# The last group's first layer as seven products of quarters, with shared sums passed between PSUM banks

## The chip, the cores and the metric

The kernel runs on one core of one Trainium2 chip. Its engines work side by side and meet only at semaphores: TensorE (PE, matrix products; PEld is its weight load), VectorE (DVE), ScalarE (ACT), GpSimd (POOL) and SyncE (SP), whose queues also issue transfers. The metric is the time of one execution on the device in microseconds. TensorE writes its products into PSUM, which has eight banks of 512 f32 values per partition; VectorE and ScalarE read them from there and also can write there. SBUF is the working memory.

## What is computed

An attention with a window of 128 tokens and a linear bias (8 batches, 8 heads, 576 tokens, head size 64), whose output is the input of a normalisation and a two-layer network with a residual:

```python
scores = scale * np.matmul(q, k.transpose(0, 1, 3, 2))
mask = (rel >= 0) & (rel < window)
scores = np.where(mask, scores + bias[None], -1000000000.0)
attn = softmax(scores)
x = (attn @ v).transpose(0, 2, 1, 3).reshape(B, S, H * D)    # 8 x 576 x 512

mu, var = x.mean(-1), ((x - mu) ** 2).mean(-1)
xn = (x - mu) / np.sqrt(var + 1e-06) * g_ln
out = x + np.maximum(xn @ w_ch1, 0.0) @ w_ch2                # 512 -> 2048 -> 512
```

## The kernel before

The 8 x 576 tokens are cut into 36 blocks of 128: two batches form a pair, a pair has nine blocks, and block 8 of a pair holds the two 64-token tails (T = 8). The blocks go through the network in groups: four groups of two blocks and then seven of four (groups 4 to 10). Group 10, the last one, has four blocks, 512 tokens.

TensorE's work is written out in order by hand. `weave_at` runs the generator of one layer of one group and, at listed places, lets attention steps of later blocks in between (scores, exponentials, masks, products with v, centring, transposes). Within a queue every engine works in the order of the program. The last group has no attention left to weave in.

**First layer (`mlp1`, L724).** The centred input stands transposed in `turned_x[g]` as four row blocks (NKB = 4) of 512 tokens. For each of 16 column blocks of w1 (NFB = 16), four matmuls of 512 columns accumulate into one PSUM bank (L734), and ScalarE (L750) or, for blocks 6 and 13 of a group, VectorE (L742) writes the ReLU of it to `ht_all` as f16. `w1g` is w1 with the gain of the normalisation multiplied in. Dividing by the standard deviation is left to the end (`rstd`, from `inv_std`, L590, nine small VectorE steps in a chain).

**Second layer by seven products (`mlp2_seven`, L813, and `mlp2_last`, L892).** From group 4 on the product of the hidden layer and w2 is made from seven products of quarters in place of eight. The hidden layer A is cut into quarters by tokens and by hidden blocks, w2 (B) by hidden blocks and by output columns. Four sums of quarters of A (`sum_hidden`, L794, on VectorE, into `hsums`) and four of B (`sum_w2`, once) enter the products. Some products accumulate on top of others in one bank: the bank is read by `onto` (scaled by `rstd` and added to the output) and then the next product is added to what is in it. A sum that two quarters of the output share is made in this way once. For the last group `mlp2_last` does the same per half of the tokens (`pair`), in pieces of 256 columns: 14 products of 8 matmuls (L905), each followed by an `onto` (L919) and, where a half row of the output is complete, by a store.

The places where `sum_hidden` runs during the first layer are in `SUMS_AT` (by unit of the first layer). The last group's `inv_std` runs after unit 1 of its first layer.

**PSUM.** Two score tiles take four banks (`ps_scores`), and a pool of four buffers (`ps_mm`) serves everything else. **Buffers.** `raw_pool` has four buffers each for q and k as loaded (1024 f16 values per partition), `turned_pool` holds them transposed (four for q, five for k). Once the last block's attention is done, none of them is used any more.

Of the kernel before, what the change touches and what calls it, by code (L numbers as in the profile page):

```python
# [53 lines left out]
}  # L54

FAR = 60000.0


# [20 lines left out]
def kernel(  # L79
# [21 lines left out]
    def pool(name, bufs, **kw):  # L101
        return ctx.enter_context(tc.tile_pool(name=name, bufs=bufs, **kw))

    consts = pool("consts", 1)
    raw_pool = pool("raw", 4)
    turned_pool = {"q": pool("turned_q", 4), "k": pool("turned_k", 5)}
# [4 lines left out]
    group_pool = pool("group", 3)  # L111
    out_pool = pool("outp", 5)
    sums_pool = pool("sums", 1)
    ps_scores = pool("ps_scores", 1, space=PSUM)
    ps_mm = pool("ps_mm", 4, space=PSUM)


    iden_dram = nc.inline_tensor(np.eye(P, dtype=np.float16), name="iden16")
# [605 lines left out]
    def mlp1(g, on_dve=()):  # L724
        xT = turned_x[g]
        w = w1 if g < FIRST_GROUPS else w1g
        cols = len(members[g]) * P

        at = g % 2 * cols if len(members[g]) == 2 else 0
        ht = hidden[g] = ht_all[:, :, at : at + cols]  # L730
        for fb in range(NFB):
            ps = ps_mm.tile([P, 4 * P], FP32, tag="mm", name="ps_m1")
            for kb in range(NKB):
                nc.tensor.matmul(  # L734
                    ps[:, 0:cols],
                    w[:, kb, fb * P : (fb + 1) * P],
                    xT[:, kb, 0:cols],
                    start=(kb == 0),
                    stop=(kb == NKB - 1),
                )  # L740
            if fb in on_dve:
                nc.vector.tensor_scalar(  # L742
                    out=ht[:, fb, :],
                    in0=ps[:, 0:cols],
                    scalar1=0.0,
                    scalar2=None,
                    op0=ALU.max,
                )
            else:
                nc.scalar.activation(  # L750
                    out=ht[:, fb, :], in_=ps[:, 0:cols], func=AF.Relu
                )
            yield cols
# [29 lines left out]
    def minus(out, a, b, op=ALU.subtract):  # L783
        nc.vector.tensor_tensor(out=out, in0=a, in1=b, op=op)  # L784

    def sum_w2(i):
# [2 lines left out]
        out, a, b = [(t1, b12, b11), (t3, b22, b12), (t2, b22, t1), (t4, b21, t2)][i % 4]  # L789
        minus(out[:, c], a[:, c], b[:, c])  # L790

    hsums = {}
# [99 lines left out]
    def mlp2_last(g):  # L892


        ht = hidden[g]
        s = [hsums.pop((g, i)) for i in (1, 2, 3, 4)]
        a11, a12, a22 = ht[:, 0:half], ht[:, half:NFB], ht[:, half:NFB]
        outs = {}

        def quarter():  # L900
            return ps_mm.tile([P, DM], FP32, tag="mm", name="ps_q")[:, 0 : DM // 2]

        def product(ps, lhs, at, rhs, first):
            for fb in range(half):
                nc.tensor.matmul(  # L905
                    ps,
                    lhs[:, fb, at : at + P],
                    rhs[:, fb, :],
                    start=(first and fb == 0),
                    stop=(fb == half - 1),  # L910
                    skip_group_check=True,
                )

        def onto(ps, at, cols, fresh):
            p, blk = members[g][at]
            n = p * NSLOT + blk
            if at not in outs:
                outs[at] = out_pool.tile([P, DM], FP32, tag="o", name="o")
            nc.vector.scalar_tensor_tensor(  # L919
                out=outs[at][:, cols],  # L920
                in0=ps,
                scalar=rstd[:, n : n + 1],
                in1=(xs[p, blk] if fresh else outs[at])[:, cols],
                op0=ALU.mult,
                op1=ALU.add,
            )

        x = {}
        for pair in range(2):
            x[pair] = quarter()  # L930
            product(x[pair], a11, pair * P, b11, True)
            onto(x[pair], pair, left, True)
            yield
        for pair in range(2):
            t = quarter()
            product(t, a12, pair * P, b21, True)
            onto(t, pair, left, False)
            yield
        for pair in range(2):
            top, low = pair, 2 + pair  # L940
            at = pair * P
            product(x[pair], s[1], at, t2, False)
            onto(x[pair], top, right, True)
            yield
            y = quarter()
            product(y, s[0], at, t1, True)
            onto(y, low, right, True)
            yield
            product(x[pair], s[2], at, t3, False)
# [3 lines left out]
            product(y, s[3], at, b22, False)  # L953
            onto(y, top, right, False)
            store(*members[g][top], outs[top])
# [16 lines left out]
        )  # L972
        store(p, blk, o)

    def store(p, blk, o, cols=slice(0, DM)):
        n = p * NSLOT + blk
        for b, t0, w, p0 in spans(p, blk):
            dst, src = out[b, t0 : t0 + w, cols], o[p0 : p0 + w, cols]
            if blk == T:
                last = n >= count - 4 and b % 2 == 1  # L980
                (nc.scalar if last else nc.sync).dma_start(out=dst, in_=src)
            else:
                dst = dst.rearrange("(c r) d -> r c d", r=2)
                last = n >= count - 4
                for r in range(2):
                    (nc.scalar if last and r else nc.sync).dma_start(
                        out=dst[r], in_=src[r * HALF : (r + 1) * HALF]
                    )

    def weave_at(units, *places, seven=None, sums=None):  # L990


        advance_to(done + places.count(-1))
        for u, _ in enumerate(units):
            if seven is not None:
# [18 lines left out]
    with tc.manual_schedule(engines={engine.PE}):  # L1014
        with tc.manual_schedule(engines={engine.Activation, engine.DVE, engine.SP, engine.Pool}):
            advance_to(first)
            weave_at(mlp1(0, (0, 1)), 2, 7, 8, 9, 13)
            weave_at(mlp1(1), 2, 8, 12)
            weave_at(mlp2(0, ((0, 8), (8, 12), (12, NFB))), 1, 4, 8, 10, 10, 12)
            weave_at(mlp2(1), 1, 3, 5, 7, 9, 13, 13)  # L1020
            weave_at(mlp1(2), 0, 4, 7, 9, 14)
            weave_at(mlp2(2), 1, 5, 9, 13, 13, 15, 15)

            weave_at(mlp1(3, (9, 10, 11)), 4, 7, 8, 10, 12, 15, sums=0)
            weave_at(mlp2(3), 0, 2, 3, 6, 9, 11, sums=4)
            for g in range(4, len(GROUPS)):
                one, two = LEAD[g - 4]
                weave_at(mlp1(g, (6, 13) if one else ()), *one, seven=g)  # L1030
                last = g == len(GROUPS) - 1
                weave_at((mlp2_last if last else mlp2_seven)(g), *two)
    assert done == len(steps)


# [28 lines left out]
```

## Time and profile before

| | |
|---|---|
| median of three runs | 309.07 us (309.05 to 312.04) |
| profiled execution | 309.11 us, span 307.3 us |
| TensorE busy | 299.2 us, 97% of the span |
| VectorE / ScalarE / GpSimd busy | 231.7 / 182.2 / 111.9 us |
| last group's first layer | 277.10 to 290.91 us |
| last group's second layer | 290.91 to 303.30 us |
| last VectorE instruction | ends at 303.82 us |

Times in the rows are microseconds from the start of the span, and a row of the timeline gives start, length, engine, line, operation, tiles, shape and count; in square brackets stands the idle time of the engine before it and what ended that. A row of the groups gives the count, the busy time, the mean length of one in ns, and the idle time before them. Since matmuls are pipelined, the length of one is longer than its share of the time: what a matmul costs in a row is the distance between starts.

### The profile page before, as it was taken

To read this page: it belongs to the slowest core of one execution; us is meant where nothing else is said; L and a number is where in the kernel's file an instruction comes from. 1 tells how busy PE (TensorE), PEld (TensorE's weight loads), DVE (VectorE), ACT (ScalarE), POOL (GpSimd) and SP (SyncE) were. 2 spreads that over 40 slices of the span, in tenths; PEclk is the share of its full clock that TensorE was granted. 3 is DMA by queue.
4 is the path that set the end of the run, shared out by engine and by line. 5 is a ranking of instruction groups with operands and counts; after the bars stand their busy time and mean duration, and the time that the engine had idled before them with its cause. 6 is when DMAs were issued, how large, how long until landed. Compare 5 with 4: busy or idle time off the path is not lost.

```text
span 307.3 us, 9098 instructions
## 1 busy us (share of the span) xinstructions
PE 299.2 (97%) x3734; PEld 198.9 (65%) x3734; DVE 231.7 (75%) x624; ACT 182.2 (59%) x327; POOL 111.9 (36%) x152
## 2 busy tenths in 40 slices
PE   8889999999999999999999999999999999999994
PEld 2468755856754578647855786568646864784583
DVE  2688878789986799669867986798679867963563
ACT  7588775768967862675268536753685368305600
POOL 8923648583775372484117350750000000000000
PEclk9999999999999999999999999999999999999999
DMA  9999999999999999999999999994741161005004
GB/s 112 165 206 200 190 159 143 200 116 122 154 123 189 146 132 134 217 152 139 117 182 123 110 134 162 127 151 77 139 89 34 20 138 35 19 19 137 0 19 120
DMA packets 149851, 38.02 MB, mean 124 GB/s; under 512 B 140721, under 2 KB 145457, under 8 KB 149810
## 3 DMA queue, kind: packets, MB, share of 16 engines
q0 software_dynamic: 103744, 18.36, 87.4%
q1 hardware_dynamic: 45586, 18.56, 36.6%
q8 instruction: 29, 0.48, 0.7%
q10 hardware_dynamic: 480, 0.52, 0.5%
q14 instruction: 12, 0.10, 0.1%
HBM read 36.90 MB, written 9.44 MB: 151 GB/s over the span
## 4 chain that ended last, share of the span: by engine, by line
PE 89%; DMA 4%; POOL 3%; ACT 1%; issue 1%; DVE 0%; POOLq 0%
PE ps_m L734 39%; PE ps_s L826 25%; PE ps_m L764 9%; PE ps_sc L418 6%; DMA w<-in_moe_w_ch_dram 4%; PE ps_sc L500 4%; PE ps_q L905 4%; POOL vx L246 1%; POOL q L211 1%; POOL w L172 1%; POOL k L211 1%; PE ps_pv L471 1%; PE ps_tr L305 1%; PE ps_tx L571 1%; PE ps_sc L305 0%
## 5 line engine op out<-in xcount | busy, mean ns | idle before, releaser
L734 PE MATMUL ps_m<-xT,w1g 128*128 128x512 f16 (+1 forms) x576 | 117.8, 356 | 0.1
L750 ACT ACTIVATE ht_all<-ps_m 128x512 f16<-128x512 f32 (+1 forms) x159 | 81.2, 519 | 38.0 <-PE ps_m L734 36.0
L734 PEld LDWEIGHTS <-w1g 128*128 128x128 f16 x576 | 53.9, 98 | 49.9 <-issue 0.3
L426 ACT ACTIVATE probs<-ps_sc 128x1024 f16<-128x1024 f32 x56 | 56.5, 1029 | 46.2 <-PE ps_sc L418 46.2
L246 POOL DMA_DIRECT2D vx<-in_v_dram x40 | 34.0, 860 | 64.2 <-PE ps_sc L500 38.7
L826 PE MATMUL ps_s<-w,s 128*128 128x256 f16 x384 | 43.8, 273 | 0.0
L826 PEld LDWEIGHTS <-s 128*128 128x128 f16 x384 | 36.7, 98 | 4.7
L437 DVE TENSOR_TENSOR probs<-probs,m 128x1024 f16<-128x1024 f16 x56 | 36.9, 683 | 2.8 <-ACT probs L426 2.8
L826 PE MATMUL ps_s<-w,ht_all 128*128 128x256 f16 x288 | 34.3, 273 | 0.0
L784 DVE TENSOR_TENSOR s<-ht_all 128x1024 f16<-128x1024 f16 (+2 forms) x35 | 20.4, 583 | 18.1 <-ACT ht_all L750 17.5
L764 PE MATMUL ps_m<-w,ht_all 128*128 128x512 f16 x128 | 31.4, 380 | 0.0
L826 PEld LDWEIGHTS <-ht_all 128*128 128x128 f16 x288 | 27.3, 98 | 5.0
L235 POOL DMA_DIRECT2D q<-in_q_dram x40 | 27.5, 702 | 5.6 <-DMA vx<-in_v_dram 2.4
L847 DVE SCALAR_TENSOR_TENSOR o<-ps_s,rstd,x 128x256 f32<-128x256 f32 x48 | 21.0, 478 | 10.5 <-PE ps_s L826 10.5
L418 PE MATMUL ps_sc<-q,k 64*64 64x128 f16 (+1 forms) x1088 | 24.1, 210 | 1.0 <-ACT probs L426 0.8
L418 PEld LDWEIGHTS <-k 64*64 64x64 f16 x1088 | 15.8, 107 | 13.0 <-issue 10.5
L582 ACT ACTIVATE junk<-xc 128x512 f16<-128x512 f16 x28 | 17.6, 628 | 5.7 <-DVE xc L551 5.6
L232 POOL DMA_DIRECT2D k<-in_k_dram x20 | 18.0, 915 | 6.3 <-DMA k<-k 5.0
L509 DVE SCALAR_TENSOR_TENSOR x<-ps_sc,rec 128x512 f16<-128x512 f32 x28 | 19.4, 691 | 1.0
L847 DVE SCALAR_TENSOR_TENSOR o<-ps_s,rstd,o 128x256 f32<-128x256 f32 x36 | 15.7, 478 | 4.2 <-PE ps_s L826 4.0
L764 PEld LDWEIGHTS <-ht_all 128*128 128x128 f16 x128 | 11.1, 98 | 10.8
L500 PEld LDWEIGHTS <-probs 128*128 128x128 f16 x352 | 14.6, 98 | 3.5
(88 smaller groups left out, 327.1 us busy)
## 6 DMA issues: line engine op xcount, KB each, us to landing
out_dram<-o SPq DMA_DIRECT2D x66, 128.0 KB, 2.4
k<-in_k_dram POOLq DMA_DIRECT2D x32, 128.0 KB, 7.2
vx<-in_v_dram POOLq DMA_DIRECT2D x32, 128.0 KB, 7.1
w<-in_moe_w_ch_dram POOLq DMA_DIRECT2D x8, 512.0 KB, 10.9
q<-in_q_dram POOLq DMA_DIRECT2D x48, 64.0 KB, 6.1
q<-in_q_dram POOLq DMA_DIRECT2D x12, 128.0 KB, 7.7
k<-in_k_dram POOLq DMA_DIRECT2D x8, 64.0 KB, 6.8
vx<-in_v_dram POOLq DMA_DIRECT2D x8, 64.0 KB, 5.8
```

The costliest lines, as they stand in the source:

```text
L235: nc.gpsimd.dma_start(out=t[half, b], in_=tokens.rearrange("h (c r) d -> r c h d", r=2)[r],)
L246: nc.gpsimd.dma_start(out=vx[p0 : p0 + n, :, 0:D], in_=v[b, :, t0 : t0 + n, :].rearrange("h p d -> p h d"),)
L418: nc.tensor.matmul(in_halves(ps[cols, j, n, t, :])[:, r, queries], kt[rows, hp, cols], in_halves(qt[rows, b, hp])[:, r, queries], start=Tr ...
L426: nc.scalar.activation(out=dst.rearrange("p (n j) q -> p j n q", j=2), in_=ps.rearrange("p j n t q -> p j n (t q)"), func=AF.Exp, scale=in ...
L437: nc.vector.tensor_tensor(out=dst, in0=dst, in1=mask, op=ALU.mult)
L500: nc.tensor.matmul(ps[:, h, 0 : D + 1], pr[:, h, t, :], vext[(p * NSLOT + o) % NV][:, h, :], start=(n == 0), stop=(n == len(terms) - 1),)
L734: nc.tensor.matmul(ps[:, 0:cols], w[:, kb, fb * P : (fb + 1) * P], xT[:, kb, 0:cols], start=(kb == 0), stop=(kb == NKB - 1),)
L750: nc.scalar.activation(out=ht[:, fb, :], in_=ps[:, 0:cols], func=AF.Relu)
L764: nc.tensor.matmul(sums[at], ht[:, fb, at * P : (at + 1) * P], w2[:, fb, :], start=(fb == 0), stop=(fb == NFB - 1),)
L784: nc.vector.tensor_tensor(out=out, in0=a, in1=b, op=op)
L826: nc.tensor.matmul(ps[:, pair, :], lhs[:, fb, at : at + P], rhs[:, fb, :], start=(first and pair == 0 and fb == 0), stop=(fb == half - 1), ...
L847: nc.vector.scalar_tensor_tensor(out=outs[at][:, cols], in0=ps[:, pair], scalar=rstd[:, n : n + 1], in1=(xs[p, blk] if fresh else outs[at] ...
```

## The change

The last group's first layer is now made of seven products of quarters as well (`mlp1_last` replaces `mlp1` there). A is w1 (with gain), cut by input rows (row blocks 0, 1 and 2, 3) and by hidden columns (low and high 1024); B is the transposed input, cut by input rows and by tokens (256 and 256). A unit u is two of the eight column blocks of a half; it makes both its blocks of either half of the hidden layer, for all tokens. Each product of a unit is two blocks times two row blocks, four matmuls of 256 columns, into one bank. Per unit there are seven products, 28 matmuls, and there are four units.

- `a1`: a11 b11 into a bank x; ScalarE copies x into a second bank t (PSUM to PSUM).
- `a2`: a product of sums into a bank y; ScalarE copies y to SBUF as f32 (`copied`).
- `b`: a product of sums on top of x; VectorE writes x + copied to a bank s. A product on top of t completes the first quarter; ScalarE writes its ReLU.
- `c`: a product of sums on top of x; VectorE writes x + copied to `ht_all` (`out`, not yet clipped). A product on top of s completes the second quarter; ReLU on ScalarE (units 0, 2) or VectorE (units 1, 3).
- `d`: a product on top of x completes the third quarter; ReLU on ScalarE. VectorE clips the fourth in place, and then makes `sum_hidden` 1 and 2 for the unit.

x has three banks in turn, y one, t and s two each: all eight. For this the scores' banks are given back before the last group, and the pool `ps_mm` is opened first.

w1's eight sums (four for each of two row blocks, 128x1024 f16) are made on VectorE in groups 7, 8 and 9, into the raw buffers of q and k. The four sums of the input (128x512 f16) and `inv_std` come during the second layer of group 9, after units 20, 24 and 26.

In the second layer the order changes: the first product goes between `c` and `d` of the first layer's last unit, the four products with sums 1 and 2 come for both halves of the tokens before those with sums 3 and 4, and `sum_hidden` 3 and 4 run during it, in halves (128x1024). Each half row of the first two blocks is stored when it is done, the first halves from SP alone.

```diff
+W1_SUMS_AT = {
+    7: ({}, {25: 0}),
+    8: ({5: 4, 8: 1, 11: 5}, {25: 2}),
+    9: ({5: 6, 8: 3, 11: 7}, {}),
 }
...
+    def sum_w1(i):
+        kb, which = i // 4, i % 4 + 1
+        t = raw_pool.tile([P, FFN // 2], FP16, tag="qk"[kb], name="w1s")
+        w1sums[which, kb] = t
+        a11, a21 = w1g[:, kb, 0 : FFN // 2], w1g[:, kb, FFN // 2 :]
+        a12, a22 = w1g[:, 2 + kb, 0 : FFN // 2], w1g[:, 2 + kb, FFN // 2 :]
+        if which == 1:
+            minus(t, a21, a22, ALU.add)
+        elif which == 2:
+            minus(t, w1sums[1, kb], a11)
+        elif which == 3:
+            minus(t, a11, a21)
+        else:
+            minus(t, a12, w1sums[2, kb])
...
+    def mlp1_last(g, between, ps_last):
...
+        def a1(u):
+            product(x_of[u % 3], u, (0, 0), b11, True)
+            nc.scalar.copy(out=t_of[u % 2], in_=x_of[u % 3])
+
+        def a2(u):
+            product(y, u, 1, xsums[1], True)
+            c = turned_pool["q"].tile([P, 8 * P], FP16, tag="q", name="c")
+            copied[u] = c.bitcast(FP32)
+            nc.scalar.copy(out=copied[u], in_=y)
+
+        def b(u):
+            product(x_of[u % 3], u, 2, xsums[2], False)
+            minus(s_of[u % 2], x_of[u % 3], copied[u], ALU.add)
+            product(t_of[u % 2], u, (2, 0), b21, False)
+            nc.scalar.activation(out=out(u, 0, 0), in_=two(t_of[u % 2]), func=AF.Relu)
+
+        def c(u):
+            product(x_of[u % 3], u, 3, xsums[3], False)
+            minus(out(u, 1, 1), two(x_of[u % 3]), two(copied[u]), ALU.add)
+            product(s_of[u % 2], u, 4, b22, False)
+            if u % 2:
+                at_least_0(out(u, 0, 1), two(s_of[u % 2]))
+            else:
+                nc.scalar.activation(out=out(u, 0, 1), in_=two(s_of[u % 2]), func=AF.Relu)
+
+        def d(u):
+            product(x_of[u % 3], u, (2, 1), xsums[4], False)
+            nc.scalar.activation(out=out(u, 1, 0), in_=two(x_of[u % 3]), func=AF.Relu)
+            at_least_0(out(u, 1, 1), out(u, 1, 1))
+            units = 2 * u, 2 * u + 2
+            sum_hidden(g, 1, units)
+            sum_hidden(g, 2, units)
...
+        a1(0)
+        a2(0)
+        a1(1)
+        b(0)
+        a2(1)
+        a1(2)
+        for u in range(n):
+            if 0 < u < n - 1:
+                if u > 1:
+                    a1(u + 1)
+                a2(u + 1)
+            c(u)
+            if u < n - 1:
+                b(u + 1)
+            else:
+                between()
+            d(u)
...
+                if g == last - 1:
+                    late[20] = [(sum_x, last, i) for i in (1, 2)]
+                    late[24] = [(sum_x, last, i) for i in (3, 4)]
+                    late[26] = [(inv_std, sum(GROUPS[:last]), len(members[last]))]
...
+            units = mlp2_last(last)
+            scores_psum.close()
+            ps_last = pool("ps_last", 1, space=PSUM)
+            LAST_SUMS_AT = {
+                u: [(sum_hidden, last, 3 + u % 2, (c, c + half // 2))]
+                for u, c in ((2, 0), (4, half // 2), (3, 0), (5, half // 2))
+            }
+            mlp1_last(last, lambda: next(units), ps_last)
+            weave_at(units, more=LAST_SUMS_AT)
```

More of the change, by code (lines that the diff above doesn't have):

```diff
@@ L102, in pool @@
         return ctx.enter_context(tc.tile_pool(name=name, bufs=bufs, **kw))
+    ps_mm = pool("ps_mm", 4, space=PSUM)
     consts = pool("consts", 1)
@@ new lines, in mlp1_last, with product, two, out @@
+    def mlp1_last(g, between, ps_last):
+        xT = turned_x[g]
+        mid = 2 * P
+        ht = hidden[g] = ht_all
+        b11, b21, b22 = xT[:, 0:2, 0:mid], xT[:, 2:4, 0:mid], xT[:, 2:4, mid:]
+        *x_of, y = (
+            ps_last.tile([P, 4 * P], FP32, name=f"ps_x{i}", tag=f"ps_x{i}") for i in range(4)
+        )
+        t_of, s_of = (
+            [ps_mm.tile([P, 4 * P], FP32, tag="mm", name=f"ps_{n}") for _ in range(2)]
+            for n in "ts"
+        )
+        copied = {}
+        def product(ps, u, kbs, rhs, fresh):
+            for j in range(2):
+                for kb in range(2):
+                    fb = 2 * u + j
+                    if isinstance(kbs, tuple):
+                        first, low = kbs
+                        w = w1g[:, first + kb, (8 * low + fb) * P :][:, 0:P]
+                    else:
+                        w = w1sums[kbs, kb][:, fb * P : (fb + 1) * P]
+                    nc.tensor.matmul(
+                        ps[:, j * mid : (j + 1) * mid],
+                        w,
+                        rhs[:, kb, :],
+                        start=(fresh and j == 0 and kb == 0),
+                        stop=(kb == 1),
+                        skip_group_check=True,
+                    )
+        def two(ps):
+            return ps.rearrange("p (f c) -> p f c", f=2)
+        def out(u, low, second):
+            return ht[:, 8 * low + 2 * u : 8 * low + 2 * u + 2, second * mid : (second + 1) * mid]
+        def a1(u):
[17 more added lines that the diff above has]
+                at_least_0(out(u, 0, 1), two(s_of[u % 2]))
+            else:
+                nc.scalar.activation(out=out(u, 0, 1), in_=two(s_of[u % 2]), func=AF.Relu)
[6 more added lines that the diff above has]
+            sum_hidden(g, 2, units)
+        def at_least_0(out, ps):
+            nc.vector.tensor_scalar(
+                out=out, in0=ps, scalar1=0.0, scalar2=None, op0=ALU.max
+            )
+        n = NFB // 4
+        a1(0)
[12 more added lines that the diff above has]
+                b(u + 1)
+            else:
+                between()
+            d(u)
@@ L937, in mlp2_last @@
             onto(t, pair, left, False)
+            store(*members[g][pair], outs[pair], left, (nc.sync, nc.sync))
+            yield
+        y = {}
+        for pair in range(2):
+            top, low = pair, 2 + pair
+            at = pair * P
+            product(x[pair], hsums[g, 2], at, t2, False)
+            onto(x[pair], top, right, True)
+            yield
+            y[pair] = quarter()
+            product(y[pair], hsums[g, 1], at, t1, True)
+            onto(y[pair], low, right, True)
             yield
@@ L941, in mlp2_last @@
             at = pair * P
[L942 to L949, printed above, removed]
+            product(x[pair], hsums[g, 3], at, t3, False)
             onto(x[pair], low, right, False)
@@ L952, in mlp2_last @@
             yield
-            product(y, s[3], at, b22, False)
-            onto(y, top, right, False)
-            store(*members[g][top], outs[top])
+            product(y[pair], hsums[g, 4], at, b22, False)
+            onto(y[pair], top, right, False)
+            store(*members[g][top], outs[top], right)
             yield
@@ L979, in store, with weave_at @@
             if blk == T:
-                last = n >= count - 4 and b % 2 == 1
-                (nc.scalar if last else nc.sync).dma_start(out=dst, in_=src)
+                two[b % 2].dma_start(out=dst, in_=src)
             else:
                 dst = dst.rearrange("(c r) d -> r c d", r=2)
-                last = n >= count - 4
                 for r in range(2):
-                    (nc.scalar if last and r else nc.sync).dma_start(
+                    two[r].dma_start(
                         out=dst[r], in_=src[r * HALF : (r + 1) * HALF]
                     )
-    def weave_at(units, *places, seven=None, sums=None):
+    def weave_at(units, *places, seven=None, sums=None, more={}):
         advance_to(done + places.count(-1))
         for u, _ in enumerate(units):
+            for f, *args in more.get(u, []):
+                f(*args)
             if seven is not None:
```

36 lines of the change are left out of this document (28 added, 8 removed).

## The prediction

> **What bounds the kernel now.** I read the head of the page first, then the end of the chain of waits, then the last 30 us on the timeline and by windows.
>
> ```profile
> span 307.3 us, 9098 instructions
> PE 299.2 (97%) x3734; PEld 198.9 (65%) x3734; DVE 231.7 (75%) x624; ACT 182.2 (59%) x327; POOL 111.9 (36%) x152
> ...
> 268.53 8.73 PE ps_s L826 x80
> 277.26 13.81 PE ps_m L734 x64
> 291.07 12.24 PE ps_q L905 x112
> 303.34 0.48 DVE o L919
> ...
> 277.10:290.91 13.81, 13.81 (x67) 6.25 (x64) 6.17 (x18) 8.96 (x15) 0.00 (x0) 1.00 0.33 76
> 290.91:303.30 12.39, 12.39 (x113) 10.85 (x111) 8.08 (x18) 0.60 (x1) 0.00 (x0) 1.00 0.16 44
> ```
>
> TensorE is busy for 97% of the span, and the chain ends in TensorE alone: the last group's first layer (L734), its second (L905), one VectorE instruction and the stores. The windows (columns: length, PE, PEld, DVE, ACT, POOL, granted clock) show both layers without a TensorE gap at full clock. In the first, VectorE works 6.17 us of 13.81 and ScalarE 8.96; that is the room the change spends. The profiled execution took 309.11 us, its span 307.3; the median of the runs is 309.07, so I sum against 309.11.
>
> **The products.** Each form's price is its spacing in a long row.
>
> ```profile
> 290.91 3.66 PE L905 MATMUL ps_q<-w,ht_all 128*128 128x256 f16 x32
> 294.40 3.66 PE L905 MATMUL ps_q<-w,s 128*128 128x256 f16 x32
> ...
> L905 PEld LDWEIGHTS <-s 128*128 128x128 f16 x64 | 6.3, 98 | 0.7
> ```
>
> First layer before: 64 matmuls of 512 columns in 13.81 us, 0.2158 each. After: 7 products x 16 matmuls of 256 columns = 112. That form takes (294.40 - 290.91)/32 = 0.109 us, and its 98 ns weight load fits beneath. 112 x 0.1092 = 12.23 us, a saving of **1.58 us** if TensorE never waits. The second layer keeps its 112 matmuls and its last three products in the same order, so the tail behind the last product stays.
>
> **w1's sums.** Eight VectorE sums of 128x1024 f16 go into groups 7 to 9, 0.60 us of queue each (0.69 long, overlapping the next by about 0.09). They stand just ahead of these idle times:
>
> ```profile
> 217.24 0.88 DVE L847 SCALAR_TENSOR_TENSOR o<-ps_s,rstd,x 128x256 f32<-128x256 f32 x2 [1.28 <-PE ps_s L826]
> 226.07 0.69 DVE L784 TENSOR_TENSOR s<-ht_all 128x1024 f16<-128x1024 f16 x1 [1.20 <-ACT ht_all L750]
> 228.66 0.56 DVE L784 TENSOR_TENSOR s<-ht_all 128x768 f16<-128x768 f16 x1 [0.70 <-ACT ht_all L750]
> 248.48 0.88 DVE L847 SCALAR_TENSOR_TENSOR o<-ps_s,rstd,x 128x256 f32<-128x256 f32 x2 [1.28 <-PE ps_s L826]
> 257.21 0.69 DVE L784 TENSOR_TENSOR s<-ht_all 128x1024 f16<-128x1024 f16 x1 [1.15 <-ACT ht_all L750]
> 259.80 0.56 DVE L784 TENSOR_TENSOR s<-ht_all 128x768 f16<-128x768 f16 x1 [0.69 <-ACT ht_all L750]
> ...
> 233.22 1.19 SPq L338 DMA_TRANSPOSE q<-q x1
> ```
>
> One sum falls ahead of 217.24, two ahead of 226.07, one ahead of 228.66, one ahead of 248.48, two ahead of 257.21, one ahead of 259.80: 4.8 us into 6.30 us of idle, and only 257.21 is over, by 0.05. **Cost 0**; without this cover they would cost up to 4.8. Each sum also waits for its raw buffer: the last transpose out of one is issued at 233.22, and the sum that takes that buffer stands near 256, so nothing queued behind it is held. The evictions of block 6 (L742) move back by up to 0.6 us; their bank is next written three blocks, 3 x 4 x 0.2158 = 2.6 us, later.
>
> **The start of the new layer.** x's sums and inv_std move ahead of group 9's last pair of `onto` on VectorE, and the first shared sum stands behind all of it.
>
> ```profile
> 275.55 0.88 DVE L847 SCALAR_TENSOR_TENSOR o<-ps_s,rstd,o 128x256 f32<-128x256 f32 x2 [0.87 <-PE ps_s L826]
> 277.30 0.88 DVE L847 SCALAR_TENSOR_TENSOR o<-ps_s,rstd,x 128x256 f32<-128x256 f32 x2 [0.87 <-PE ps_s L826]
> 278.09 0.16 DVE L596 TENSOR_SCALAR aa<-moments 128x4 f32<-128x4 f32 x1
> 279.66 0.16 DVE L614 SCALAR_TENSOR_TENSOR rstd<-hh,rstd 128x4 f32<-128x4 f32 x1
> ...
> L784 DVE TENSOR_TENSOR s<-s,ht_all 128x512 f16<-128x512 f16 x1 | 0.4, 426 | 0.0
> ```
>
> The first two sums of x (two of 0.426 plus 0.04 between dependent ones) fill the 0.87 idle before 275.55. Then the queue is: pair until 276.34 (a pair takes 278.09 - 277.30 = 0.79), sums 3 and 4 until 277.26, inv_std's nine steps (279.82 - 278.09 and a gap: 1.77) until 279.03, the last pair until 279.82, then the shared sum s of unit 0. TensorE meanwhile does a1(0), a2(0), a1(1), b(0), a2(1), a1(2): 28 matmuls, 277.10 + 3.06 = 280.16. Then c(0) writes into the bank that the shared sum is reading.
>
> **The price of a shared sum** (f32 PSUM plus f32 SBUF, 128x512) is in no row. The nearest:
>
> ```profile
> L509 DVE SCALAR_TENSOR_TENSOR x<-ps_sc,rec 128x512 f16<-128x512 f32 x11 | 7.6, 691 | 0.4
> L742 DVE TENSOR_SCALAR ht_all<-ps_m 128x512 f16<-128x512 f32 x6 | 4.1, 690 | 0.0
> L919 DVE SCALAR_TENSOR_TENSOR o<-ps_q,rstd,x 128x256 f32<-128x256 f32 x8 | 3.8, 482 | 2.3 <-PE ps_q L905 2.3
> L551 DVE TENSOR_SCALAR xc<-x,mean 128x512 f16<-128x512 f16 x11 | 3.9, 354 | 0.4
> 262.89 0.69 DVE L742 TENSOR_SCALAR ht_all<-ps_m 128x512 f16<-128x512 f32 x1
> 263.68 0.56 DVE L784 TENSOR_TENSOR s<-ht_all 128x768 f16<-128x768 f16 x1
> ```
>
> Bounds: 0.43 (512 f16 from SBUF, above) and 0.88 (two 256-column f32 instructions back to back, at 277.30). I take 0.71, a little over the two rows of 512 f32 elements from PSUM (0.69), because here the second operand is a full f32 tensor. [...]
>
> **The handovers.** TensorE to VectorE and back:
>
> ```profile
> 302.26 1.04 PE L905 MATMUL ps_q<-w,ht_all 128*128 128x256 f16 x8
> ...
> 75.81 0.28 ACT ht_all L750
> 76.14 0.60 PE ps_m L734 x4
> ```
>
> The eighth matmul starts at 302.26 + 7 x 0.109 = 303.02, and VectorE (303.34) follows 0.32 later; from an engine's end to TensorE's start it is 76.14 - 76.09 = 0.05. So s of unit 0 ends at 279.82 + 0.71 = 280.53, c(0) starts at 280.58: a stall of **0.42**.
>
> From there to d(3) TensorE has 88 matmuls, 9.61 us, and would arrive at 290.19. VectorE's second sum for unit 0 (out) starts at 280.58 + 0.33 + 0.32 = 281.23. Until d(3)'s bank is read it does seven shared sums (7 x 0.71, less six overlaps of 0.08: 4.49), one max from PSUM (0.69 - 0.08 = 0.61), three in-place maxima (0.35 each, 1.05), six hidden-layer sums (0.46 each, 2.76), three gaps of 0.10 behind an instruction whose result is read next (as 262.89 to 263.68 has it), and 0.24 waiting for b(1)'s product: 9.45, so 290.68, and d(3) at 290.73: **0.54** more. The units 1 and 3 are the ones over TensorE's 3.06 us, since they have the extra max; the wait falls in unit 3, which has no unit behind it to catch up.
>
> ScalarE has 18 steps (eight copies, ten ReLUs).
>
> ```profile
> L750 ACT ACTIVATE ht_all<-ps_m 128x512 f16<-128x512 f32 x16 | 9.6, 597 | 11.1 <-PE ps_m L734 11.1
> L426 ACT ACTIVATE probs<-ps_sc 128x1024 f16<-128x1024 f32 x14 | 14.3, 1023 | 18.0 <-PE ps_sc L418 18.0
> ```
>
> At 0.60 that is 10.8 of 12.2 us, at most five steps or 3.0 in a unit's 3.06. The copy from PSUM to PSUM is in no row: between 0.50 and 1.02 (L426's 1024 elements). At 1.02, b(0) would wait 0.4 for the first copy, but that time comes off the 0.42 wait for VectorE, so I count **0**.
>
> **Second layer.** Its third and fourth sums (four of 0.69) now stand between the `onto`s. Sum plus `onto` is about 1.0 per product of 0.87 us, four times: 0.5 behind, then products with one `onto` each. They are needed three products later: **0**; uncovered, 0.5. The early stores put four more issues on SP, which is waiting there anyway: **0**. The four banks taken over from the scores were last read by the last block's values, before 270: **0**.
>
> Sum: -1.58 + 0.42 + 0.54 = -0.62, so 309.11 - 0.62 = 308.49.
>
> **Rivals.**
> *VectorE keeps up.* With shared sums at 0.43 the start stall is 0.14 and d(3) waits for nothing: -1.44, 307.7. For it: VectorE's 6.17 busy of 13.81. Against: the two PSUM rows at 0.69. Chance 0.12.
> *VectorE becomes the bound and the layer is slower than before.* Of the eight shared sums seven lie on the path (the wait of 0.24 takes one up), so each 0.01 us of a sum adds 0.07; with 0.88 it is +0.57, 309.7, and past 0.88, at 1.0, 310.5. It decides at 0.80. For it: a full f32 operand and a PSUM output that no VectorE row has; the chain x, s, x, out, x within one bank. Chance 0.25.
> *w1's sums are not hidden*, because the idle places differ or a sum holds a mask that TensorE needs: -0.62 + 4.8 = +4.2, 313.3 at worst. Against: the six rows. Chance 0.04.
> *TensorE does not gain*: 256-column products with weight loads exposed, at 0.123 (0.2158 x 64/112) or more; then 310.1. Against: L905's 0.109 without gaps. Chance 0.02.
>
> **How the numbers follow.** The forecast has 0.57 (308.1 to 309.0, from sums of 0.66 to 0.78). The range must leave out no more than 2 in 10: from 307.7 (VectorE keeps up) to 310.1. One per cent, what a measurement here can tell from no change, is 3.1 us. No saving above 1.58 us is in the change: faster by over 1% 0.02. Slower by over 1% takes w1's sums uncovered, or a shared sum far past 1 us: 0.04. Within 1%: 0.94.
>
> **What the profile afterwards would show.** Right: 112 matmuls of 256 columns at 0.109 in the new layer, TensorE waiting about 0.4 at c(0) and 0.5 in unit 3, both put down to VectorE; shared sums near 0.7; no TensorE gap between 200 and 277; last product about 0.6 earlier. Wrong: waits for ScalarE's copies, a shared sum above 0.8 or below 0.6, gaps in groups 8 and 9, or waits in the second layer.

## The result, and the profile after

Over 22 runs each, taken side by side, the changed kernel has a median of 308.47 us (307.33 to 310.63) and the kernel before 309.85 us (308.62 to 312.54). The medians differ by 1.38 us. The ratio (of the means) is 0.9947, with a 95% interval of 0.9925 to 0.9969: 1.64 us less, between 0.96 and 2.3. That is inside the one per cent that counts as no change here, and its sign is told. The forecast was 0.62 us less. The profiled execution took 307.49 us with a span of 305.7, against 309.11 and 307.3.

The head of the page after, and the chain of waits from the start of the last group on (start, length, what):

```profile
span 305.7 us, 9273 instructions
PE 297.9 (97%) x3782; PEld 203.6 (67%) x3782; DVE 245.7 (80%) x651; ACT 182.4 (60%) x329; POOL 111.7 (37%) x152
...
287.57 1.02 PE ps_x L870 x8
...
289.90 0.47 PE ps_x L870 x4
290.37 11.37 PE ps_q L1055 x104
...
301.76 0.48 DVE o L1069
```

TensorE is still busy for 97% and still carries the chain to the end. VectorE has 14 us more work, and the chain meets it only in the last instruction, as before. Two of the pieces shown are longer than their matmuls cost at 0.1092 each: eight at 287.57 take 1.02 in place of 0.87, four at 289.90 take 0.47 in place of 0.44.

The windows of the last three groups before the new layer, and of the last stretch, from TensorE's first matmul of the last group to the end of its last product. The first fence is the kernel before and the second the kernel after, where the stretch is cut at 290.21, the start of the products behind d(3) (columns as in the prediction, with the DMA share and GB/s at the end):

```profile
186.55:277.10 90.55, 90.55 (x994) 60.94 (x992) 70.24 (x183) 49.24 (x82) 10.38 (x14) 1.00 0.62 83
277.10:303.30 26.20, 26.20 (x178) 17.11 (x175) 14.25 (x35) 9.55 (x16) 0.00 (x0) 1.00 0.25 61
```

```profile
186.33:276.88 90.55, 90.55 (x994) 60.97 (x992) 76.35 (x196) 49.23 (x82) 10.37 (x14) 1.00 0.62 83
276.88:290.21 13.33, 13.33 (x123) 11.71 (x121) 11.54 (x30) 9.06 (x17) 0.00 (x0) 1.00 0.35 81
290.21:301.73 11.52, 11.51 (x106) 10.07 (x103) 9.13 (x21) 0.60 (x1) 0.00 (x0) 1.00 0.23 58
```

Groups 7 to 9 take 90.55 us in both, although VectorE has 6.1 us more to do there (76.35 against 70.24). The last stretch falls from 26.20 to 13.33 + 11.52 = 24.85, by 1.35. Behind it the span has 4.0 us left in both (307.3 - 303.30 and 305.7 - 301.73). What remains of the span's 1.6 us lies ahead of 186 us: the window of group 7 starts at 186.33 after and at 186.55 before. There the kernels issue the same instructions, and this start moves from one execution to the next, as the experiments show (186.3 to 188.2 for the same instructions). So traces are compared by the two stretches, and the spans and single times are not; the 1.35 lies inside the interval of the ratio.

The same place on TensorE's timeline shows what the new layer waits for:

```profile
276.88 0.60 PE L870 MATMUL ps_x<-xT,w1g 128*128 128x256 f16 x4
...
279.50 0.60 PE L870 MATMUL ps_x<-xT,w1g 128*128 128x256 f16 x4
279.99 0.60 PE L870 MATMUL ps_x<-xs,w1s 128*128 128x256 f16 x4
...
286.53 0.60 PE L870 MATMUL ps_x<-xs,w1s 128*128 128x256 f16 x4
...
287.41 0.60 PE L870 MATMUL ps_x<-xs,w1g 128*128 128x256 f16 x4
287.99 0.60 PE L870 MATMUL ps_x<-xs,w1s 128*128 128x256 f16 x4
...
288.86 1.04 PE L1055 MATMUL ps_q<-w,ht_all 128*128 128x256 f16 x8
289.77 0.60 PE L870 MATMUL ps_x<-xs,w1g 128*128 128x256 f16 x4
290.21 2.78 PE L1055 MATMUL ps_q<-w,ht_all 128*128 128x256 f16 x24
```

Four matmuls last 0.60 but cost 0.44: the six products from 276.88 to 279.50 take 2.62, that is 24 x 0.1092. Where the distance to the next row is more than 0.44 (0.87 for eight), TensorE waited: 0.06 at c(0) (279.99), 0.14 at c(3) (287.99), 0.04 at d(3) (289.77), 0.24 in all. With the saving of 1.58 that gives -1.34, and the stretch has -1.35.

VectorE at the same places:

```profile
276.12 0.41 DVE L796 TENSOR_TENSOR xs<-xT 128x512 f16<-128x512 f16 x1
276.46 0.42 DVE L796 TENSOR_TENSOR xs<-xT,xs 128x512 f16<-128x512 f16 x1
276.79 0.16 DVE L608 TENSOR_SCALAR aa<-moments 128x4 f32<-128x4 f32 x1
...
278.46 0.87 DVE L997 SCALAR_TENSOR_TENSOR o<-ps_s,rstd,x 128x256 f32<-128x256 f32 x2
279.24 0.69 DVE L796 TENSOR_TENSOR ps_s<-ps_x,c 128x512 f32<-128x512 f32 x1
280.62 0.69 DVE L796 TENSOR_TENSOR ht_all<-ps_x,c 128x512 f16<-128x512 f32 x1 [0.69 <-PE ps_x L870]
...
282.16 0.28 DVE L919 TENSOR_SCALAR ht_all<-ht_all 128x512 f16<-128x512 f16 x1
...
283.35 0.68 DVE L796 TENSOR_TENSOR ht_all<-ps_x,c 128x512 f16<-128x512 f32 x1
...
287.24 0.70 DVE L796 TENSOR_TENSOR ps_s<-ps_x,c 128x512 f32<-128x512 f32 x1 [0.25 <-PE ps_x L870]
...
289.04 0.68 DVE L796 TENSOR_TENSOR ht_all<-ps_x,c 128x512 f16<-128x512 f32 x1
```

A shared sum takes 0.69, to PSUM or to SBUF. The first one ends at 279.93 and c(0) follows at 279.99. The brackets tell more: ahead of the sum at 287.24 VectorE stood idle for 0.25 us, waiting for TensorE's product b(3), and TensorE then waited 0.14 for that sum. Both waited in turn for one another there. That is the length of a way from engine to engine and back, and not a lack of VectorE time. At d(3) VectorE comes straight from its queue, without idle time from 287.24 to 289.72. These 2.48 us of work are shorter than the 24 matmuls (2.62) that TensorE has between b(3)'s product, whose successor starts at 286.97, and d(3). But VectorE starts 0.27 behind 286.97, and TensorE 0.05 behind VectorE's end: 2.80 in all, 0.18 more than 2.62, and this is the wait of c(3) and d(3) together.

### The profile page after: what moved, and what is told of

Read it like the earlier page. It is cut to its first block, busy times and chain, and to the rows that moved or that the text cites. A ratio compares the mean times of both kernels' runs of the same rounds, so it can differ in the third digit from the quotient of the medians.

```text
span 305.7 us, 9273 instructions
## 1 busy us (share of the span) xinstructions
PE 297.9 (97%) x3782; PEld 203.6 (67%) x3782; DVE 245.7 (80%) x651; ACT 182.4 (60%) x329; POOL 111.7 (37%) x152
## 4 chain that ended last, share of the span: by engine, by line
PE 90%; DMA 5%; POOL 2%; ACT 2%; issue 1%; DVE 0%; ACTq 0%; POOLq 0%
PE ps_m L746 36%; PE ps_s L976 25%; PE ps_m L776 9%; PE ps_sc L430 6%; PE ps_sc L512 4%; PE ps_q L1055 4%; PE ps_x L870 3%; DMA q<-q 3%; DMA k<-in_k_dram 2%; PE ps_pv L483 1%; POOL q L223 1%; ACT probs L438 1%; PE ps_tr L317 1%; PE ps_sc L317 1%; POOL vx L258 1%
## 5 line engine op out<-in xcount | busy, mean ns | idle before, releaser
L746 PE MATMUL ps_m<-xT,w1g 128*128 128x512 f16 (+1 forms) x512 | 103.8, 353 | 0.0
L762 ACT ACTIVATE ht_all<-ps_m 128x512 f16<-128x512 f32 (+1 forms) x143 | 71.7, 511 | 26.5 <-PE ps_m L746 24.5
L746 PEld LDWEIGHTS <-w1g 128*128 128x128 f16 x512 | 47.6, 98 | 42.6 <-issue 0.4
```

The costliest lines, as they stand in the source:

```text
L746: nc.tensor.matmul(ps[:, 0:cols], w[:, kb, fb * P : (fb + 1) * P], xT[:, kb, 0:cols], start=(kb == 0), stop=(kb == NKB - 1),)
L762: nc.scalar.activation(out=ht[:, fb, :], in_=ps[:, 0:cols], func=AF.Relu)
```

## The experiments

The theory after the traces: the whole gain is TensorE's 1.58 us, less 0.24 us of waits for VectorE. The sums of w1 lie in VectorE's idle time and cost nothing. The second layer's new order earns nothing by itself, but it lets the hidden sums 3 and 4 leave the first layer, where VectorE has no room for them. The rivals, run by run, stand in the expectations. "Stretch" is the last group on TensorE (26.20 before, 24.85 after), "groups 7 to 9" the one ahead of it (90.55 in both).

**The order alone.** The kernel before, with the second layer's new order and the new stores:

```diff
+        y = {}
         for pair in range(2):
...
-            product(x[pair], s[1], at, t2, False)
+            product(x[pair], hsums[g, 2], at, t2, False)
...
-            y = quarter()
-            product(y, s[0], at, t1, True)
-            onto(y, low, right, True)
+            y[pair] = quarter()
+            product(y[pair], hsums[g, 1], at, t1, True)
+            onto(y[pair], low, right, True)
             yield
-            product(x[pair], s[2], at, t3, False)
+        for pair in range(2):
+            top, low = pair, 2 + pair
+            at = pair * P
+            product(x[pair], hsums[g, 3], at, t3, False)
...
```

> The kernel before with only the new order of the second layer, its third and fourth sums still made during the old first layer, and the new stores. Measured on the last stretch, from TensorE's first instruction of the last group's first layer to the end of its last product: 26.20 us before (277.10 to 303.30), 24.85 after (276.88 to 301.73). Theory (the gain is TensorE's shorter first layer, 1.58, less 0.24 of waits): the order costs and brings nothing, 26.2, time as before. Rival (a part of the gain is the order's or the stores'): 25.2 to 26.0, or a shorter tail behind the last product than 4.0 us.

Measured: stretch 26.21, groups 7 to 9 90.55, and 3.99 us behind the stretch; ratio to the kernel before 1.0007 (0.9978 to 1.0036). So the order and the stores are worth nothing by themselves.

**The sums alone.** The kernel before with the additions to VectorE ahead of the last group: w1's eight sums, the input's four, and `inv_std` moved there. Nothing uses the sums.

```diff
...
+                if g == last - 1:
+                    late[20] = [(sum_x, last, i) for i in (1, 2)]
+                    late[24] = [(sum_x, last, i) for i in (3, 4)]
+                    late[26] = [(inv_std, sum(GROUPS[:last]), len(members[last]))]
+                weave_at(mlp1(g, (6, 13) if one else ()), *one, seven=g, more=early)
+                weave_at((mlp2_last if g == last else mlp2_seven)(g), *two, more=late)
...
```

> The kernel before, old first and second layer, with w1's eight sums, the input's four and the earlier inv_std on VectorE; the sums are made and not used. Theory (they fit into VectorE's idle time): groups 7 to 9, from 186.55 to the start of the last group, stay at 90.55 us without a TensorE wait, and the last stretch at 26.2; time as before. Rival (they delay masks or evictions that TensorE waits for): up to 4.8 us more in groups 7 to 9.

Measured: groups 7 to 9 90.54, stretch 26.21; ratio 0.9987 (0.9963 to 1.0012). All of it is hidden.

**How much cover there is.** The changed kernel with each of w1's sums made twice, into the same buffer (`again_w1` does what `sum_w1` does, without taking a new buffer):

```diff
...
-                early, late = ({u: [(sum_w1, i)] for u, i in at.items()} for at in W1_SUMS_AT.get(g, ({}, {})))
+                early, late = ({u: [(sum_w1, i), (again_w1, i)] for u, i in at.items()} for at in W1_SUMS_AT.get(g, ({}, {})))
```

> The changed kernel with each of w1's eight sums made twice, 4.8 us more on VectorE in groups 7 to 9; the result is the same. Theory (their cover is VectorE's idle time, 6.3 us at their places): 9.6 us don't fit, TensorE waits for masks, sums or evictions, groups 7 to 9 grow from 90.55 by 0.5 to 3.3 us. Rival (VectorE's lag does not reach TensorE there at all): 90.55.

The window of groups 7 to 9, and TensorE's timeline there, where brackets stand in two rows:

```profile
187.44:280.76 93.32, 90.87 (x993) 61.17 (x992) 81.16 (x204) 49.47 (x82) 10.37 (x14) 1.00 0.61 81
```

```profile
240.26 5.40 PE L991 MATMUL ps_s<-w,s 128*128 128x256 f16 x48 [1.07 <-DVE o L1012]
271.25 0.20 PE L512 MATMUL ps_sc<-vx,own 128*128 128x65 f16 x1 [1.38 <-DVE own L449]
```

Measured: 93.32, 2.77 more, with TensorE idle for 2.45 of it: 1.07 behind an `onto` and 1.38 behind a mask, both of them queued on VectorE behind the doubled sums (VectorE is busy for 81.16 there, against 76.35 in the changed kernel). The stretch stays at 24.84; the ratio is 1.0044 (1.0026 to 1.0062). So 4.8 us of sums fit and 9.6 don't. This fits the 6.30 us of idle time that the prediction counted: 9.6 is 3.3 over, and 2.77 came.

**The hidden sums back in the first layer.** The changed kernel with sums 3 and 4 made in each unit rather than in the second layer:

```diff
             sum_hidden(g, 2, units)
+            sum_hidden(g, 3, units)
+            sum_hidden(g, 4, units)
...
-            weave_at(units, more=LAST_SUMS_AT)
+            weave_at(units)
```

> The changed kernel, but with the hidden layer's third and fourth sums made in each unit of the first layer (128x512) instead of during the second. Theory (VectorE is nearly full in the new layer: 0.49 us idle from 280.62 to 289.72): six more sums of 0.45 stand ahead of the last unit's shared sum, 2.7 - 0.5 = 2.2 more of waits, last stretch 27.0, slower than before by 0.8. Rival (VectorE has room, TensorE alone sets the layer): 24.9 to 25.3.

TensorE's timeline of this run:

```profile
284.92 0.60 PE L870 MATMUL ps_t<-xT,w1g 128*128 128x256 f16 x4
285.76 0.60 PE L870 MATMUL ps_x<-xs,w1g 128*128 128x256 f16 x4 [0.24 <-DVE ht_all L796]
...
288.38 0.60 PE L870 MATMUL ps_t<-xT,w1g 128*128 128x256 f16 x4
289.35 0.60 PE L870 MATMUL ps_x<-xs,w1g 128*128 128x256 f16 x4 [0.37 <-DVE ht_all L796]
...
290.82 1.04 PE L1057 MATMUL ps_q<-w,ht_all 128*128 128x256 f16 x8
292.40 0.60 PE L870 MATMUL ps_x<-xs,w1g 128*128 128x256 f16 x4 [0.54 <-DVE ht_all L796]
```

(A bracket counts from the modelled end of the matmul ahead. By the starts, the waits are 0.40, 0.53 and 0.70.) Measured: stretch 26.45, 1.60 more than the changed kernel, so the whole gain is gone; ratio to the kernel before 0.9985 (0.9948 to 1.0022). Here VectorE is short of time: TensorE waits for it at every d from unit 1 on, and longer each time, where the changed kernel waits 0.04 at d(3) alone. The theory had a larger loss, so the direction and the place hold, and the size was too high.

**The same with the old order.** Sums 3 and 4 in the units, and the second layer and its stores as before (its first product still goes ahead of d(3)):

```diff
...
-            y[pair] = quarter()
-            product(y[pair], hsums[g, 1], at, t1, True)
-            onto(y[pair], low, right, True)
+            y = quarter()
+            product(y, hsums[g, 1], at, t1, True)
+            onto(y, low, right, True)
             yield
-        for pair in range(2):
-            top, low = pair, 2 + pair
-            at = pair * P
...
```

> As the run with the sums in the units, and with the second layer's old order and stores as well. Theory (the order itself is worth nothing, only the place of the sums is): 27.0, within 0.2 of the run with the sums in the units. Rival (the order is worth something of its own): more than 0.3 longer than that run.

Measured: stretch 26.46, ratio 0.9987 (0.9963 to 1.0010): the run above to 0.01. With the sums in the first layer, too, the order is worth nothing by itself.

**What a shared sum costs.** Each shared sum as two VectorE instructions of 256 columns:

```diff
-            minus(s_of[u % 2], x_of[u % 3], copied[u], ALU.add)
+            for j in (slice(0, mid), slice(mid, 2 * mid)):
+                minus(s_of[u % 2][:, j], x_of[u % 3][:, j], copied[u][:, j], ALU.add)
...
-            minus(out(u, 1, 1), two(x_of[u % 3]), two(copied[u]), ALU.add)
+            for j in range(2):
+                minus(out(u, 1, 1)[:, j], two(x_of[u % 3])[:, j], two(copied[u])[:, j], ALU.add)
```

> The changed kernel with each of the eight shared sums made as two VectorE instructions of 256 columns, so that one costs about 0.88 us in place of 0.69. Theory (VectorE's price of a shared sum decides, seven of eight lie on the path, 0.49 us of idle is left): 0.17 more at c(0) and 7 x 0.19 - 0.49 = 0.84 more before d(3), last stretch 24.85 + 1.0 = 25.9. Rival (TensorE alone sets the layer): 24.9 to 25.1.

VectorE's timeline of this run, the first two shared sums, and TensorE's at c(3):

```profile
279.66 0.89 DVE L796 TENSOR_TENSOR ps_s<-ps_x,c 128x256 f32<-128x256 f32 x2
281.23 0.76 DVE L796 TENSOR_TENSOR ht_all<-ps_x,c 128x256 f16<-128x256 f32 x2 [0.69 <-PE ps_x L870]
```

```profile
288.96 0.60 PE L870 MATMUL ps_x<-xs,w1s 128*128 128x256 f16 x4 [0.21 <-DVE ps_s L796]
```

Measured: stretch 25.46, 0.61 more than the changed kernel and between theory and rival; ratio 0.9962 (0.9946 to 0.9977). Halving a sum to PSUM costs 0.20 (0.89 against 0.69), but one to SBUF only 0.07 (0.76 against 0.69), so four of the eight sums grew by less than was reckoned. Even so TensorE waits longer: 0.24 at c(0), 0.37 at c(3), 0.11 at d(3), against 0.06, 0.14 and 0.04, and 0.09 ahead of or within c(2), where there was none. The idle time of VectorE ahead of the sum that c(3) waits for is gone in this run, so with sums of this length its work does become the limit.

**The start alone.** `inv_std` made twice ahead of the last group, 1.67 us more on VectorE ahead of the first shared sum:

```diff
-                    late[26] = [(inv_std, sum(GROUPS[:last]), len(members[last]))]
+                    late[26] = [(inv_std, sum(GROUPS[:last]), len(members[last]))] * 2
```

> The changed kernel with inv_std done twice ahead of the last group, 1.67 us more on VectorE before the first shared sum; the result is the same. Theory (the nine small steps stand ahead of the shared sum that c(0) waits for): c(0) waits 1.7 instead of 0.06, everything behind moves with it, last stretch 26.5. Rival 1 (VectorE catches up in its idle 0.49): 26.0 to 26.1. Rival 2 (the wait at c(0) has another cause): 24.9.

```profile
281.64 0.60 PE L870 MATMUL ps_x<-xs,w1s 128*128 128x256 f16 x4 [1.55 <-DVE ps_s L796]
```

Measured: stretch 26.51, 1.66 more; ratio 0.9998 (0.9976 to 1.0020). The layer starts at the same 276.88 as in the changed kernel, and c(0) comes at 281.64 rather than 279.99. VectorE's queue up to the first shared sum is thus a term of the sum without any slack: what is added there is added to the stretch, and the waits further on stay as they were (0.15 and 0.04). It would alone have eaten the gain.

**The second layer's first products as cover.** The first product goes ahead of c(3), the second between c(3) and d(3):

```diff
         for u in range(n):
...
+            if u == n - 1:
+                between()
             c(u)
...
-                u: [(sum_hidden, last, 3 + u % 2, (c, c + half // 2))]
-                for u, c in ((2, 0), (4, half // 2), (3, 0), (5, half // 2))
+                u: [(sum_hidden, last, 3 + (u - 1) % 2, (c, c + half // 2))]
+                for u, c in ((1, 0), (3, half // 2), (2, 0), (4, half // 2))
```

> The changed kernel with the second layer's first product ahead of c(3) and its second between c(3) and d(3), so that TensorE has 0.87 us of other work in both places where it waits for VectorE in the last unit (0.14 and 0.04). Theory: both waits go, last stretch 24.85 - 0.18 = 24.67; too little for the times to tell. Rival (the wait moves to the next handover, to ScalarE's ReLU that the first product needs): 24.8 to 25.0.

The timeline of this run behind c(3): the last three rows of TensorE before the hidden sums are used, ScalarE's last ReLU, and the weight load that has a bracket:

```profile
291.49 1.04 PE L1057 MATMUL ps_q<-w,ht_all 128*128 128x256 f16 x8
292.36 0.60 PE L870 MATMUL ps_x<-xs,w1g 128*128 128x256 f16 x4
292.80 2.12 PE L1057 MATMUL ps_q<-w,ht_all 128*128 128x256 f16 x16
293.00 0.60 ACT L912 ACTIVATE ht_all<-ps_x 128x512 f16<-128x512 f32 x1 [2.35 <-PE ps_x L870]
293.65 0.99 PEld L1057 LDWEIGHTS <-ht_all 128*128 128x128 f16 x10 [0.31 <-ACT ht_all L912]
```

Measured: stretch 24.87; ratio 0.9947 (0.9921 to 0.9973). The waits at c(3) and d(3) are gone (292.36 is 0.87 behind 291.49). But the third product stands right behind d(3) now, and its last two weights are columns that d(3) has just made: after six loads the next one waits until ScalarE's ReLU has ended at 293.60. The 16 matmuls from 292.80 to the next row at 294.75 take 1.95 and not 1.75. So 0.18 was saved and 0.20 spent at the next handover. In this execution the layer starts at 278.78, 1.9 us later than in the changed kernel's, with groups 7 to 9 at 90.54: that is the start of the kernel, which both share.

**Cover at all three places.** The first two products cut in two: four matmuls ahead of c(3), eight between c(3) and d(3), four behind d(3).

```diff
         for u in range(n):
...
+            if u == n - 1:
+                between()
             c(u)
             if u < n - 1:
                 b(u + 1)
             else:
                 between()
+                between()
             d(u)
...
-            product(x[pair], a11, pair * P, b11, True)
+            product(x[pair], a11, pair * P, b11, True, range(half // 2))
+            yield
+            product(x[pair], a11, pair * P, b11, True, range(half // 2, half))
```

> In the run with both of the second layer's first products moved, the waits at c(3) and d(3) went but 0.20 came back inside the second layer's third product: its last two weight loads wait for ScalarE's ReLU of d(3), which ends 0.8 after d(3) does, and only 6 matmuls (0.66) stood in between. Here the first product is cut in two (4 matmuls ahead of c(3), 4 behind it) and so is the second (4 ahead of d(3), 4 behind it), so 10 matmuls (1.09) cover the ReLU and 8 still stand between c(3) and d(3). Nothing is left out or added. Theory (handovers set these waits, nothing is short of throughput): no wait at c(3), d(3) nor in the second layer, last stretch 112 and 112 matmuls at 0.1092 and the last one's end, 24.63 to 24.70, against 24.85. Rival (VectorE is the bound there, its work has to be done before the second layer's sums): the waits only move again and the stretch stays 24.8 to 24.9. In the time 0.05 per cent, which the rounds can't tell: the ratio should be that of the changed kernel, 0.992 to 0.997.

```profile
277.44 0.60 PE L870 MATMUL ps_x<-xT,w1g 128*128 128x256 f16 x4
...
288.40 0.60 PE L1058 MATMUL ps_q<-w,ht_all 128*128 128x256 f16 x4
288.83 0.60 PE L870 MATMUL ps_x<-xs,w1s 128*128 128x256 f16 x4
...
289.71 1.04 PE L1058 MATMUL ps_q<-w,ht_all 128*128 128x256 f16 x8
290.58 0.60 PE L870 MATMUL ps_x<-xs,w1g 128*128 128x256 f16 x4
291.02 2.35 PE L1058 MATMUL ps_q<-w,ht_all 128*128 128x256 f16 x20
293.20 5.40 PE L1058 MATMUL ps_q<-w,s 128*128 128x256 f16 x48
...
301.06 1.04 PE L1058 MATMUL ps_q<-w,ht_all 128*128 128x256 f16 x8
```

Measured: stretch 24.66 (301.06 + 1.04 - 277.44), 0.19 less than the changed kernel; ratio to the kernel before 0.9953 (0.9919 to 0.9987). Every row stands at the distance of its matmuls: 0.44 for four, 0.87 for eight, 2.18 for 20. All that is left over 224 matmuls at 0.1092 is 0.04 at c(0) and the end of the last matmul. The same VectorE work, in the same order, costs nothing here, so the waits at c(3) and d(3) came from where TensorE's work stood, and not from a lack of VectorE time. By the times this version can't be told from the changed kernel; by the stretch it is the shortest of all.

## Why the prediction was right, and where it was off

**The direction and what carries it: right.** The new layer's matmuls cost 0.1092 each, as taken from the second layer's rows, and the saving of 1.58 is there in full. TensorE stays the bound.

**w1's sums at 0: right, and shown.** The sums alone leave groups 7 to 9 at 90.54; doubled, they cost 2.77. The rival in which they lie open did not come.

**The second layer at 0: right.** Its 104 matmuls behind d(3) stand in one piece of the chain (11.37 us, 104 x 0.1093). The order alone changes nothing. What the prediction did not price is what moving sums 3 and 4 out of the first layer is worth: there they cost 1.60 (shown with either order). That the new order is needed for it is not shown. Before, the product with sum 3 came two products behind the one with sum 2, and in the new order four, which leaves more time for the sums; but the old order with sums 3 and 4 made during the second layer wasn't tried.

**ScalarE at 0 and the tail unchanged: right.** The copy from PSUM to PSUM, in no row before, takes 0.57 to 0.61, nearer the lower bound of 0.50, which was the author's estimate, than the upper of 1.02. No TensorE wait falls on a copy: the three of 0.06, 0.14 and 0.04 end 0.05 to 0.06 behind a VectorE sum (279.93, 287.94, 289.72). Nor do the banks taken over from the scores cost anything: the 16 matmuls ahead of the new layer take 1.75 (275.13 to 276.88), as 16 at 0.1092 do.

**The two stalls, 0.42 and 0.54: the step that failed.** They measured 0.06 (c(0)) and 0.18 (0.14 at c(3) and 0.04 at d(3)): 0.24 in place of 0.96, and this is the whole difference between the forecast stretch (-0.62) and the measured one (-1.35). The steps were the right ones and the terms were too large:
- *The start, 0.36 too much.* Sums 3 and 4 of the input were taken at 0.46 each, as dependent instructions. They don't depend on each other, and pass in 0.67 together (276.12 to 276.79): 0.25. `inv_std` passes in 1.67 and not 1.77 (276.79 to 278.46), since the `onto` behind its last step is not held (it starts at 278.46, and the step ends at 278.54): 0.10. The shared sum took 0.69 and not 0.71.
- *VectorE up to d(3), 0.36 too much.* From the first `out` (280.62) to the end of the last one (289.72) it needs 9.10 and not 9.45. The shared sums and the maximum from PSUM were priced right (5.07 by the distances between starts, where 4.49 + 0.61 were set). The in-place maximum and the two hidden sums behind it were priced too high: in unit 0 they pass in 1.19 (282.16 to 283.35), where 0.35 + 0.10 + 2 x 0.46 = 1.37 were set, and in the three units in 3.54 and not 4.11. Against these 0.57 stands the idle time of 0.25 ahead of the sum that c(3) waits for, which the prediction didn't have.
- *The reason given for the second stall.* The prediction put it down to VectorE's throughput over units 1 and 3. In the trace VectorE is idle for 0.25 just ahead of the sum that c(3) waits for. Unit 3 alone has the wait because no products of a further unit stand between d(2) and c(3). The last experiment shows it: four matmuls put there take the wait away.

**The shared sum: right at 0.69, where 0.71 was taken.** It agrees with the two rows of 512 f32 elements from PSUM that stood nearest to it, L509's (0.691) and L742's (0.690); the 0.02 that the prediction set on top for the f32 operand did not show. Between the rivals the result, by its size, lies near "VectorE keeps up" (-1.44), but not by its mechanism: that rival needed sums of 0.43. The rival in which VectorE becomes the bound fell with the sum's price, 0.11 short of its point of decision. That point, 0.80, was itself set too low, since the rest of VectorE's work was priced too high: in the run with halved sums a shared sum takes 0.82 on average, and the stretch is still 0.74 below the 26.20 of before. The rival is a near one nevertheless: 1.67 us on VectorE at the start, or the two hidden sums in each unit, give the whole gain back.

**The times.** The ratio gives 1.64 us less, with an interval from 0.96 to 2.3, and the medians differ by 1.38: the stretch's 1.35 agrees with both, and the forecast's 0.62 lies outside the interval. That the forecast of 308.49 lies so near the measured 308.47 is partly chance: the three runs of the kernel before had their median at 309.07, and 22 have it at 309.85.

## What to carry to other kernels

When a second engine feeds the bound engine through one PSUM bank, price two things apart: its total work between two points, and the way there and back for each handover (0.27 and 0.05 us at c(3)). Here the first was mended by moving work away (1.60), the second by independent matmuls put into the gap (0.19), and the cover must be counted at the next handover too, where half of a moved product may be worth more than the whole (moved whole, 0.18 was saved and 0.20 spent; in halves, the stretch was 0.19 shorter). Hidden work should be laid into idle rows one by one, since the same sums made twice were no longer hidden (2.77 us more).

## What was unexpected of the hardware

- A VectorE sum of 512 f32 values with one operand in PSUM took 0.69 to 0.70 with its result to PSUM and 0.68 to 0.69 to SBUF as f16; as one instruction the two were at most 0.02 apart. In halves of 256 the two differ: 0.89 against 0.76 for the pair. Why a second instruction costs 0.20 in the one case and 0.07 in the other stays open.
- ScalarE's copies of 512 f32 values took as long to PSUM (0.57 to 0.61) as to SBUF (0.58 to 0.60) in the new layer:

```profile
277.51 0.57 ACT L887 COPY ps_t<-ps_x 128x512 f32<-128x512 f32 x1 [6.64 <-PE ps_x L870]
278.00 0.59 ACT L893 COPY c<-ps_x 128x512 f32<-128x512 f32 x1
278.47 0.61 ACT L887 COPY ps_t<-ps_x 128x512 f32<-128x512 f32 x1
```

- The same instructions up to group 7 end between 186.3 and 188.2 us in the profiled executions of these kernels, while groups 7 to 9 behind them repeat to 0.01 (apart from the run with w1's sums made twice). A gain of 1 us is read from a stretch, then, and not from a span.
